# Block-sorted attention and a StarReLU feed-forward on one core: query transposes ahead of the spread product, all spread products together, scores directly behind the first value tile

## The chip, the cores and the metric

The kernel runs on one core of one Trainium2 chip. The metric is the device time of one execution in microseconds (us). The core has five engines with queues of their own: TensorE (PE, with its weight loads as PEld), VectorE (DVE), ScalarE (ACT), GpSimd (POOL) and SyncE (SP); DMA transfers are issued here from the queues of GpSimd and SyncE.

## The reference

Queries, keys and values have 4 batches, 8 heads, 768 positions and 64 elements per head. The positions form 8 blocks of 96. A small matrix `sort_net` (8 x 8 for each batch and head) is balanced by five rounds of exponentials and of divisions by row and column sums, and then mixes the blocks of keys and values. Attention runs inside each block, and its output goes through a feed-forward layer of 512 to 2048 to 512 with a squared ReLU.

```python
for _ in range(5):
    P = P - np.max(P, axis=-1, keepdims=True)
    P = np.exp(P)
    P = P / (np.sum(P, axis=-1, keepdims=True) + 1e-09)
    P = P / (np.sum(P, axis=-2, keepdims=True) + 1e-09)
k_sorted = np.einsum('bhij,bhjcd->bhicd', P, k_b).reshape(B, H, S, D)
v_sorted = np.einsum('bhij,bhjcd->bhicd', P, v_b).reshape(B, H, S, D)
...
scores = scale * np.matmul(q_b, k_sb.transpose(0, 1, 2, 4, 3))
scores = scores - np.max(scores, axis=-1, keepdims=True)
attn = np.exp(scores)
attn = attn / (np.sum(attn, axis=-1, keepdims=True) + 1e-09)
attn_out = np.matmul(attn, v_sb)
...
x = np.ascontiguousarray(attn_out.transpose(0, 2, 1, 3)).reshape(B * S, H * D)
h = x @ w_in
r = np.maximum(h, 0.0)
g = s * (r * r) + b
out = (g @ w_out).astype(np.float32)
```

## The kernel before

The order of instructions on every engine is written out by hand: each engine works through its instructions in the order in which the code issues them, and waits only for data and for free buffers. Every tile of the on-chip accumulator memory (PSUM) comes from one of two rings: `psa` with three tiles of two halves ("banks") of 512 f32 columns, and `psb` with two tiles of one bank. A tile of a ring is written again when all readers of its former use are done.

The work falls into a front, in which batch 0 is sorted and its first half (four of the eight blocks) is attended, and a long part in which the feed-forward of one half runs on TensorE while the attention of the next halves is laid into slots between its matmuls (`ffn1`, `ffn2` and their dictionaries of slots). The front, in the order of the code:

- **Loads.** SyncE issues `sort_net` and the values of batch 0 (`v0f`, four pieces). GpSimd issues the first half of the queries of batch 0 (`load_qh(0, 0)`, L104, 384 KB), the keys of batch 0 in three pieces (L93), builds `ident` and `emat`, and then issues the input weights `wi` (L140) with the second half of the queries in four pieces between them. GpSimd's later issues wait for earlier transfers to land.
- **Warm-up.** `warm(n, w, m)` (L127) is `n` matmuls of zeros with `w` columns and `m` output rows. There are 16 of 256 columns, 108 of 96 columns and 6 of 512.
- **Balancing** (L235 to L252). The five rounds run on VectorE with the exponentials on ScalarE; between them ScalarE also rearranges the values (`permute`, L194). The result is `sn`, one row for each batch and head.
- **Spread product** (L257). One f32 matmul for each batch brings the rows of `sn` to the partitions of that batch; each shows as two passes in the trace. `spread_first` does batch 0 into a tile of `psb`. `build_pd` (L271 to L286, VectorE) makes the mixing matrix `pd` from it.
- **Query transposes** (`q_banks`, L206). 48 transposes on TensorE (L216) into two tiles `tqb` of `psb`, and two evictions (one on VectorE, one on ScalarE) to `qt`.
- **Keys.** `k_piece` twice (L292, tiles `tp`) and `k_banks` (L318, tiles `tkb`), each with the mixing matrix, evicted to `ks` by VectorE and ScalarE in turn (`evac`, L202 and L204).
- **Values and scores.** `v_piece` (L328, tiles `tv`) sorts a quarter of the values and is evicted to `vs`. Behind the first comes `spread_all`: the spread products of all four batches (eight passes) into the last 128 columns of both banks of a `psa` tile `sc1`, and a copy by ScalarE to `later` (L269), from which `build_pd` of batches 1 to 3 reads. Then come `s_banks` and `s_piece`, the scores of head pairs 0 and 1 (L398, L380) with their exponentials on ScalarE (L403, L384); the scores of pair 1 go to the same tile `sc1`. Three more `v_piece` follow; the evictions of the third and fourth are cut into two halves.
- **Product with the values** (`p_piece`, L408). It takes `fill` matmuls of zeros with 240 columns (L416), eight matmuls (L422, tile `pv`), and on VectorE a reciprocal (L427) and a multiplication (L428) to `x`. `t_piece` (L433, transposes at L439) turns `x` to `xt`, with evictions on ScalarE, and `part` (L464) begins the feed-forward (L468 fills, L473 `hps`).

The second half of the queries of batch 0 is transposed in the first slot of `ffn1(0)`.

Of the kernel before, what the change touches and what calls it, by code (L numbers as in the profile page):

```python
# [9 lines left out]
FP = mybir.dt.float32  # L10
# [12 lines left out]
def kernel(  # L23
# [12 lines left out]
    nc = tc.nc  # L36

    B, H, S, D = q.shape
    NB = sort_net.shape[-1]
# [7 lines left out]
    TG = HB * BLK  # L47
# [32 lines left out]
    for c in range(0, C2, CV):  # L80
        nc.sync.dma_start(out=v0f[:, c:c + CV, :].rearrange("p c d -> p (c d)"),
                          in_=raw[2][0][:, c * D:(c + CV) * D])
# [44 lines left out]
    def warm(n, w=512, m=128):  # L127
        z = psb.tile([128, 512], FP, tag="b", name="z")
        for _ in range(n):
            nc.tensor.matmul(out=z[0:m, 0:w], lhsT=zeros[:, 0:m], rhs=zeros[:, 0:w],  # L130
                             start=True, stop=True)
# [68 lines left out]
    def evac(eng, out, in_):  # L200
        if eng == "A":
            nc.scalar.copy(out=out, in_=in_)  # L202
        else:
            nc.vector.tensor_copy(out=out, in_=in_)  # L204

    def q_banks(b, half, engs):  # L206
        if b not in QT:
            QT[b] = trp.tile([128, 2, NHP, CQ, 64], BF, tag="qt", name="qt")
        pr = slice(half * 64, (half + 1) * 64)
        for u in range(2):  # L210
            tr = psb.tile([128, 1024], BF, tag="b", name="tqb")
            for a in range(2 * u, 2 * u + 2):
                for c in range(CQ):
                    for e in range(2):
                        o = (a % 2 * CQ + c) * 64
                        nc.tensor.transpose(out=tr[e * 64:(e + 1) * 64, o:o + 64],  # L216
                                            in_=QH[b][pr, 2 * a + e, c, :],
                                            identity=ident[pr, pr])
            evac(engs[u], QT[b][:, half, 2 * u:2 * u + 2].rearrange("p a c t -> p (a c t)"),
                 tr[:, 0:2 * TG])  # L220

    idle = [
        lambda: nc.vector.tensor_reduce(
# [6 lines left out]
    nc.vector.tensor_tensor(out=sn, in0=sn, in1=rstat.broadcast_to([BH, NB, NB]),  # L230
                            op=ALU.subtract)
    warm(16, 256)
    warm(108, 96, 64)
    warm(6)
    for it in range(5):  # L235
        nc.scalar.activation(out=sn, in_=sn, func=AF.Exp)
        for c in {1: (0,), 3: (1,), 4: (2, 3)}.get(it, ()):
# [13 lines left out]
        nc.vector.tensor_tensor(out=sn, in0=sn, in1=spread(rrec, [[0, NB], list(rrec.ap[1])]),  # L251
                                op=ALU.mult)  # L252
    PD = {}
    later = const.tile([128, 2, B // 2, NB * NB], FP)

    def spread_rows(b, o):
        nc.tensor.matmul(out=o, lhsT=emat[:, b, :], rhs=sn.rearrange("p i j -> p (i j)"),  # L257
                         start=True, stop=True)

    def spread_first():  # L260
        pe = psb.tile([128, 512], FP, tag="b", name="pe")
        spread_rows(0, pe[:, 0:NB * NB])
        return pe[:, 0:NB * NB]

    def spread_all(ps):
        for b in range(B):
            o = TG + b // 2 * NB * NB
            spread_rows(b, ps[:, b % 2, o:o + NB * NB])
        nc.scalar.copy(out=later.rearrange("p u w n -> p u (w n)"), in_=ps[:, :, TG:512])  # L269

    def build_pd(b, rows):  # L271
        tmp = rtp.tile([128, NB, NB], FP, tag="tmp", name="tmp")
        nc.vector.tensor_tensor(out=tmp, in0=rows.rearrange("p (i j) -> p i j", j=NB),
                                in1=spread(jsel, [[0, NB], list(jsel.ap[1])]), op=ALU.mult)
        pt = rtp.tile([128, NB], FP, tag="pt", name="pt")
        nc.vector.tensor_reduce(out=pt, in_=tmp, axis=AX.X, op=ALU.add)
        cs = rtp.tile([128, 1], FP, tag="cs", name="cs")
        nc.vector.tensor_reduce(out=cs, in_=pt, axis=AX.X, op=ALU.add)
        rc = rtp.tile([128, 1], FP, tag="rc", name="rc")
        nc.vector.reciprocal(out=rc, in_=cs)  # L280
        pd = const.tile([128, 2, 2, NG], BF, name=f"pd{b}")
        nc.vector.scalar_tensor_tensor(
            out=pd.rearrange("p e z (a i) -> p (e z a) i", i=NB),
            in0=spread(bm, [list(bm.ap[1]), [0, NB]]), scalar=rc,
            in1=spread(pt, [[0, 4 * NHP], list(pt.ap[1])]), op0=ALU.mult, op1=ALU.mult)
        PD[b] = pd  # L286
# [79 lines left out]
    def s_piece(b, half, hp, sc=None):  # L366
        g0 = hp * NB + half * HB
        if sc is None:
            sc = psa.tile([128, 2, 512], FP, tag="a", name="sc")
        byp = len(QT[b].shape) == 5  # L370
        for n in range(HB):
            for e in range(2):
                pr = slice(e * 64, (e + 1) * 64)
                if byp:
                    o = sc[:, e, 0:TG].rearrange("p (c t) -> p c t", c=CQ)[:, :, 16 * n:16 * n + 16]
                    r = QT[b][pr, half, hp, :, 16 * n:16 * n + 16]
                else:
                    o = sc[:, e, n * BLK:(n + 1) * BLK]
                    r = QT[b][pr, half * HB + n, hp, :]
                nc.tensor.matmul(out=o, lhsT=KS[b % 2][pr, g0 + n].rearrange("p z c -> p (z c)"),  # L380
                                 rhs=r, start=True, stop=True)
        at = atp.tile([KR, 2, TG], BF, tag="at", name="at")
        if byp:
            nc.scalar.activation(out=at.rearrange("p e (t c) -> p e t c", c=CQ),  # L384
                                 in_=sc[0:KR, :, 0:TG].rearrange("p e (c t) -> p e t c", c=CQ),
                                 func=AF.Exp, scale=scale)
        else:
            nc.scalar.activation(out=at, in_=sc[0:KR, :, 0:TG], func=AF.Exp, scale=scale)  # L388
        AT[b, half, hp] = at

    def s_banks(b, half, hp):
        g0 = hp * NB + half * HB
        at = atp.tile([KR, 2, TG], BF, tag="at", name="at")
        sc = [psb.tile([128, TG], FP, tag="b", name="scb") for _ in range(2)]
        for n in range(HB):
            for e in range(2):
                pr = slice(e * 64, (e + 1) * 64)
                nc.tensor.matmul(  # L398
                    out=sc[e].rearrange("p (c t) -> p c t", c=CQ)[:, :, 16 * n:16 * n + 16],
                    lhsT=KS[b % 2][pr, g0 + n].rearrange("p z c -> p (z c)"),  # L400
                    rhs=QT[b][pr, half, hp, :, 16 * n:16 * n + 16], start=True, stop=True)
        for e in range(2):
            nc.scalar.activation(out=at[:, e].rearrange("p (t c) -> p t c", c=CQ),  # L403
                                 in_=sc[e][0:KR].rearrange("p (c t) -> p t c", c=CQ),
                                 func=AF.Exp, scale=scale)
        AT[b, half, hp] = at

    def p_piece(b, half, hp, fill=0):  # L408
        g0 = hp * NB + half * HB
        atf = AT.pop((b, half, hp)).rearrange("p e t -> p (e t)")  # L410
        if hp == 0:
            X[b, half] = xp.tile([BLK, HB, d_model], BF, tag="x", name="x")
        x = X[b, half]
        pv = psa.tile([128, 2, 512], FP, tag="a", name="pv")
        for i in range(fill):
            nc.tensor.matmul(out=pv[:, i % 2, 272:512], lhsT=zeros[:, 0:128], rhs=zeros[:, 0:240],  # L416
                             start=True, stop=True)
        for e in range(2):
            for n in range(HB):
                c0 = (e * HB + n) * BLK  # L420
                m = 128 if c0 + 128 <= 2 * TG else BLK
                nc.tensor.matmul(out=pv[0:m, e, n * VW:(n + 1) * VW],  # L422
                                 lhsT=atf[:, c0:c0 + m], rhs=VS[b % 2][:, e * NG + g0 + n, :],
                                 start=True, stop=True)
        pvv = pv[0:BLK, :, 0:HB * VW].rearrange("p e (n w) -> p e n w", w=VW)
        rec = rtp.tile([BLK, 2, HB], FP, tag="rec", name="rec")
        nc.vector.reciprocal(out=rec, in_=pvv[:, :, :, D])  # L427
        nc.vector.tensor_tensor(  # L428
            out=x[:, :, hp * 128:(hp + 1) * 128].rearrange("p n (e d) -> p e n d", e=2),
            in0=pvv[:, :, :, 0:D],  # L430
            in1=rec.unsqueeze(3).broadcast_to([BLK, 2, HB, D]), op=ALU.mult)
# [93 lines left out]
        nc.sync.dma_start(out=out[r0:r0 + 128, ns], in_=ot[:, ns])  # L525


    build_pd(0, spread_first())
    q_banks(0, 0, "DA")
    k_piece(0, 0, "D")  # L530
    k_piece(0, CK, "A")
    k_banks(0, 2 * CK, "DA")
    v_piece(0, 0, "D")
    sc1 = psa.tile([128, 2, 512], FP, tag="a", name="sc")
    spread_all(sc1)
    s_banks(0, 0, 0)
    s_piece(0, 0, 1, sc1)
    v_piece(0, CK, "D")
    v2 = v_piece(0, 2 * CK, "D", 1)
    v3 = v_piece(0, 3 * CK, "A", 1)  # L540
    v2("D")
    s_banks(0, 0, 2)
    p_piece(0, 0, 0, 3)
    v3("A")
    p_piece(0, 0, 1, 2)
    s_banks(0, 0, 3)
# [48 lines left out]
    def VRW(b, u): return lambda: v_rows(b, u)  # L595
    def VB(b): return lambda: v_back(b)
    def TD(b, h): return lambda: t_dma(b, h)
    def PDB(b): return lambda: build_pd(b, later[:, b % 2, b // 2, :])
    def QD(b): return lambda: q_dma(b)
    def LV(b): return lambda: load("v", b, 6, QT[b - 1][:, NB - 1, 0, 0:1])  # L600

# [83 lines left out]
```

## Time and profile before

| What | us |
|---|---|
| Median of three runs | 222.98 (222.55 to 224.73) |
| Profiled execution | 222.54 |
| Its span, first to last instruction | 220.4 |
| TensorE busy, share of the span | 213.6 (97%) |
| VectorE busy | 126.0 (57%) |
| ScalarE busy | 109.4 (50%) |
| GpSimd busy | 70.8 (32%) |
| Spread product of batch 0 (L257), start | 11.23 |
| First scores (L398), start | 16.52 |
| First product with values (L422), start | 20.03 |
| First `hps` matmul (L473), start | 23.13 |

The time of the execution holds some 2 us outside the span. Starts are counted from the start of the span. A busy TensorE is not TensorE at its peak, since matmuls overlap one another and a single one shows about 0.2 us from entry to end, while the next may enter 0.016 us behind it. The idle time of an engine costs something only where the chain of work that ends last runs through it.

### The profile page before, as it was taken

Reading aid. Unit: us, or ns where it says so; the run is one execution under the profiler, and the core shown is the slowest. Engines: PE = TensorE matmul, PEld = TensorE weight load, DVE = VectorE, ACT = ScalarE, POOL = GpSimd, SP = SyncE. Lnnn points to the kernel's source line nnn. Section 1 sums busy time; section 2 is a strip of 40 time slices with the busy share of each in tenths; the row PEclk is TensorE's granted clock in tenths of the full one; section 3 lists DMA queues with packets and bytes.
Section 4 is the critical chain, followed back from the end, with each engine's and each line's share of the span. In section 5 each row is a group of like instructions: output and inputs, shape, how many; then the busy total and the mean of one; then the engine's idle time right before and its main releaser. Section 6 shows DMA issues by size and latency. Waiting matters only on the chain.

```text
span 220.4 us, 5172 instructions
## 1 busy us (share of the span) xinstructions
PE 213.6 (97%) x2156; PEld 128.8 (58%) x2175; DVE 126.0 (57%) x257; ACT 109.4 (50%) x149; POOL 70.8 (32%) x127
## 2 busy tenths in 40 slices
PE   7989999999999999999999999999999999999994
PEld 5877766555465555666446555665446566654454
DVE  6777457567875768547636677547417744441222
ACT  4677687658635445664622535665424356550000
POOL 7659781689832004920050008800000000000000
PEclk9999999999999999999999999999999999999999
DMA  6999999999979662999979846999911940001212
GB/s 154 284 164 125 120 170 204 204 172 134 128 215 181 49 187 41 178 208 121 141 204 175 107 135 88 208 179 102 215 72 48 123 119 3 0 0 48 93 53 95
DMA packets 67255, 28.92 MB, mean 131 GB/s; under 512 B 51872, under 2 KB 63264, under 8 KB 67232
## 3 DMA queue, kind: packets, MB, share of 16 engines
q0 software_dynamic: 31168, 12.85, 49.5%
q1 hardware_dynamic: 36064, 15.74, 35.6%
q8 instruction: 17, 0.28, 0.6%
q14 instruction: 6, 0.05, 0.1%
HBM read 28.85 MB, written 7.86 MB: 167 GB/s over the span
## 4 chain that ended last, share of the span: by engine, by line
PE 90%; DMA 5%; DVE 1%; issue 1%; POOL 1%; ACT 0%; POOLq 0%
PE hps L473 38%; PE ops L497 36%; DMA rawk<-in_k_dram 5%; PE pv L422 4%; PE sc L380 3%; PE tpp L302 2%; PE ops L514 2%; PE tv L328 2%; PE tvr L347 1%; DVE vs L204 1%; PE tr L439 1%; PE scb L398 1%; POOL rawk L93 0%; PE sc L257 0%; PE pv L416 0%
## 5 line engine op out<-in xcount | busy, mean ns | idle before, releaser
L473 PE MATMUL hps<-xt,wi 128*128 128x384 bf16 x512 | 87.9, 326 | 0.0
L497 PE MATMUL ops<-wo,gt 128*128 128x512 bf16 x350 | 82.4, 379 | 1.4 <-issue 0.6
L485 ACT ACTIVATE rt<-hps 128x768 bf16<-128x768 f32 x64 | 51.8, 811 | 39.5 <-PE hps L473 38.3
L473 PEld LDWEIGHTS <-wi 128*128 128x128 bf16 x512 | 49.0, 98 | 32.6 <-issue 0.4
L486 DVE TENSOR_TENSOR gt<-rt 128x768 bf16<-128x768 bf16 x64 | 36.0, 565 | 41.2 <-ACT rt L485 41.0
L497 PEld LDWEIGHTS <-gt 128*128 128x128 bf16 x368 | 34.1, 98 | 37.4
L522 DVE SCALAR_TENSOR_TENSOR ot<-ops,s_bc,bias 128x512 f32<-128x512 f32 (+2 forms) x27 | 18.6, 691 | 34.7 <-PE ops L497 31.6
L388 ACT ACTIVATE at<-sc 112x768 bf16<-112x768 f32 x24 | 18.1, 808 | 30.1 <-PE sc L380 30.1
L428 DVE TENSOR_TENSOR x<-pv,rec 96x512 bf16<-96x512 f32 x32 | 22.0, 686 | 1.1
L115 POOL DMA_DIRECT2D qtok<-in_q_dram x24 | 18.6, 808 | 0.7 <-issue 0.7
L422 PEld LDWEIGHTS <-at 112*128 112x128 bf16 (+1 forms) x256 | 12.9, 101 | 6.7 <-ACT at L388 1.0
L202 ACT CAST ks<-tpp 64x512 bf16<-64x512 f32 x18 | 13.2, 731 | 4.7 <-DVE ks L204 4.1
L140 POOL DMA_DIRECT2D wi<-in_moe_w_in_dram x24 | 12.8, 558 | 5.5 <-DMA rawk<-in_k_dram 3.2
L422 PE MATMUL pv<-vs,at 112*128 112x66 bf16 (+1 forms) x256 | 13.9, 195 | 0.1
L204 DVE CAST ks<-tpp 64x512 bf16<-64x512 f32 x18 | 13.1, 729 | 0.9 <-ACT ks L202 0.5
L93 POOL DMA_DIRECT2D rawk<-in_k_dram x21 | 11.2, 550 | 2.7 <-issue 1.9
L93 POOL DMA_DIRECT2D rawv<-in_v_dram x18 | 9.7, 558 | 6.0 <-DMA wo<-in_moe_w_out_dram 4.6
L130 PE MATMUL z<-zeros 128*64 128x96 bf16 (+2 forms) x129 | 9.8, 241 | 1.3 <-DVE zeros L118 1.2
L90 POOL COPY rawk<-xt 128x1 bf16<-128x1 bf16 x2 | 0.4, 190 | 32.8 <-DMA xt<-x 32.8
L427 DVE RECIPROCAL rec<-pv 96x8 f32<-96x8 f32 x32 | 6.4, 200 | 6.4 <-PE pv L422 6.4
L130 PEld LDWEIGHTS <-zeros 128*64 128x64 bf16 (+1 forms) x130 | 7.5, 115 | 3.0 <-DVE zeros L118 1.2
L349 DVE CAST rawv<-tvr 128x512 bf16<-128x512 f32 x12 | 8.2, 683 | 0.0
(93 smaller groups left out, 137.9 us busy)
## 6 DMA issues: line engine op xcount, KB each, us to landing
out_dram<-ot SPq DMA_DIRECT2D x22, 256.0 KB, 2.6
rawv<-in_v_dram POOLq DMA_DIRECT2D x18, 128.0 KB, 5.3
rawk<-in_k_dram POOLq DMA_DIRECT2D x18, 128.0 KB, 4.1
qtok<-in_q_dram POOLq DMA_DIRECT2D x24, 96.0 KB, 6.5
wo<-in_moe_w_out_dram POOLq DMA_DIRECT2D x4, 512.0 KB, 10.8
v0f<-in_v_dram SPq DMA_DIRECT2D x4, 384.0 KB, 5.9
vd<-rawv SPq DMA_DIRECT2D x4, 384.0 KB, 6.4
vs<-vd SPq DMA_DIRECT2D x8, 192.0 KB, 8.1
```

The costliest lines, as they stand in the source:

```text
L93: nc.gpsimd.dma_start(out=ti[:, c:c + n, :].rearrange("p c d -> p (c d)"), in_=raw["qkv".index(t)][b][:, c * D:(c + n) * D])
L115: nc.gpsimd.dma_start(out=QTOK[b][:, n], in_=qv[:, n])
L130: nc.tensor.matmul(out=z[0:m, 0:w], lhsT=zeros[:, 0:m], rhs=zeros[:, 0:w], start=True, stop=True)
L204: nc.vector.tensor_copy(out=out, in_=in_)
L388: nc.scalar.activation(out=at, in_=sc[0:KR, :, 0:TG], func=AF.Exp, scale=scale)
L422: nc.tensor.matmul(out=pv[0:m, e, n * VW:(n + 1) * VW], lhsT=atf[:, c0:c0 + m], rhs=VS[b % 2][:, e * NG + g0 + n, :], start=True, stop=True)
L428: nc.vector.tensor_tensor(out=x[:, :, hp * 128:(hp + 1) * 128].rearrange("p n (e d) -> p e n d", e=2), in0=pvv[:, :, :, 0:D], in1=rec.unsq ...
L473: nc.tensor.matmul(out=H1[t, i][:, f, 0:TG], lhsT=wi[:, hp, fc:fc + 128], rhs=XT[t][:, :, hp, :], start=(hp == 0), stop=(hp == NHP - 1))
L485: nc.scalar.activation(out=rt, in_=h, func=AF.Relu)
L486: nc.vector.tensor_tensor(out=gt[:, 2 * i:2 * i + 2, :], in0=rt, in1=rt, op=ALU.mult)
L497: nc.tensor.matmul(out=ops, lhsT=gt[:, f, m * 128:(m + 1) * 128], rhs=wo[:, f, :], start=(f == 0), stop=(f == NF - 1))
L522: nc.vector.scalar_tensor_tensor(out=ot[:, ns], in0=ops, scalar=s_bc, in1=BIAS[0][:, ns], op0=ALU.mult, op1=ALU.add)
```

## The change

`q_banks` can now return its two evictions as a list of moves instead of issuing them. The 48 query transposes of the first half are issued before the balancing loop, behind a warm-up of 16 matmuls of 256 columns and 21 of 512; behind the transposes stand 16 matmuls of zeros with 128 columns into the second bank of a new `psa` tile `pe`. `spread_first` is gone: `spread_all` brings batch 0 to the first bank of `pe` and batches 1 to 3 to the second, directly one after the other, ahead of `build_pd(0)`. The query evictions follow `build_pd(0)`, as before, and ScalarE's copy to `later` follows them, with three batches instead of four. The scores of head pairs 0 and 1 come directly behind the first `v_piece`, the second in a `psa` tile of their own. The scores of pair 2 move behind the first `p_piece`, which loses its three fills.

```diff
-    def q_banks(b, half, engs):
+    def q_banks(b, half, engs, moves=None):
...
-            evac(engs[u], QT[b][:, half, 2 * u:2 * u + 2].rearrange("p a c t -> p (a c t)"),
-                 tr[:, 0:2 * TG])
+            o = QT[b][:, half, 2 * u:2 * u + 2].rearrange("p a c t -> p (a c t)")
+            if moves is None:
+                evac(engs[u], o, tr[:, 0:2 * TG])
+            else:
+                moves.append(lambda eng=engs[u], o=o, i=tr[:, 0:2 * TG]: evac(eng, o, i))
...
     warm(16, 256)
-    warm(108, 96, 64)
-    warm(6)
+    warm(21)
+    q_moves = []
+    q_banks(0, 0, "DA", q_moves)
+    pe = psa.tile([128, 2, 512], FP, tag="a", name="pe")
+    for _ in range(16):
+        nc.tensor.matmul(out=pe[:, 1, 0:128], lhsT=zeros[:, 0:128], rhs=zeros[:, 0:128],
+                         start=True, stop=True)
     for it in range(5):
...
-    later = const.tile([128, 2, B // 2, NB * NB], FP)
+    later = const.tile([128, B - 1, NB * NB], FP)
...
-    def spread_first():
-        pe = psb.tile([128, 512], FP, tag="b", name="pe")
-        spread_rows(0, pe[:, 0:NB * NB])
-        return pe[:, 0:NB * NB]
-
-    def spread_all(ps):
+    def spread_all():
         for b in range(B):
-            o = TG + b // 2 * NB * NB
-            spread_rows(b, ps[:, b % 2, o:o + NB * NB])
-        nc.scalar.copy(out=later.rearrange("p u w n -> p u (w n)"), in_=ps[:, :, TG:512])
+            o = max(b - 1, 0) * NB * NB
+            spread_rows(b, pe[:, int(b > 0), o:o + NB * NB])
...
-    build_pd(0, spread_first())
-    q_banks(0, 0, "DA")
+    spread_all()
+    build_pd(0, pe[:, 0, 0:NB * NB])
+    for mv in q_moves:
+        mv()
+    nc.scalar.copy(out=later.rearrange("p b n -> p (b n)"), in_=pe[:, 1, 0:(B - 1) * NB * NB])
     k_piece(0, 0, "D")
     k_piece(0, CK, "A")
     k_banks(0, 2 * CK, "DA")
     v_piece(0, 0, "D")
-    sc1 = psa.tile([128, 2, 512], FP, tag="a", name="sc")
-    spread_all(sc1)
     s_banks(0, 0, 0)
-    s_piece(0, 0, 1, sc1)
+    s_piece(0, 0, 1)
     v_piece(0, CK, "D")
     v2 = v_piece(0, 2 * CK, "D", 1)
     v3 = v_piece(0, 3 * CK, "A", 1)
     v2("D")
+    p_piece(0, 0, 0)
     s_banks(0, 0, 2)
-    p_piece(0, 0, 0, 3)
     v3("A")
     p_piece(0, 0, 1, 2)
     s_banks(0, 0, 3)
...
-    def PDB(b): return lambda: build_pd(b, later[:, b % 2, b // 2, :])
+    def PDB(b): return lambda: build_pd(b, later[:, b - 1, :])
```

## The prediction

> **What bounds the kernel now.** I read the page first: the share of each engine, then the chain that ended last.
>
> ```profile
> PE 213.6 (97%) x2156; PEld 128.8 (58%) x2175; DVE 126.0 (57%) x257; ACT 109.4 (50%) x149; POOL 70.8 (32%) x127
> ...
> PE 90%; DMA 5%; DVE 1%; issue 1%; POOL 1%; ACT 0%; POOLq 0%
> ```
>
> TensorE is busy for 97% of the 220.4 us span and carries 90% of the chain; 5% of the chain (11.1 us) is the wait for the last third of the first keys, all before 14.4 us. The waits of TensorE add up to 1.2 us for the zeros at the start, 0.6 us of issue, and four stalls of 0.2 to 0.5 us, none of those four after 17.1 us. So the change, which touches only the first 22 us, is worth what it moves the point at which the dense matmuls follow one another without a gap, and nothing more. I therefore went through the timeline of the front engine by engine.
>
> ```profile
> 11.23 0.40 PE L257 MATMUL pe<-sn,emat 32*128 32x64 f32 x2 [0.22 <-DVE sn L243]
> 11.57 0.95 PE L216 MATMUL tqb<-ident,qh 64*64 64x64 bf16 x48
> 12.98 1.20 PE L292 MATMUL tp<-pd,rawk 128*64 128x64 bf16 x64 [0.47 <-DVE pd L282]
> 14.36 0.69 PE L318 MATMUL tkb<-pd,rawk 128*64 128x64 bf16 x32 [0.17 <-DMA rawk<-in_k_dram]
> ...
> 15.49 1.10 PE L257 MATMUL sc<-sn,emat 32*128 32x64 f32 x8
> 16.52 0.34 PE L398 MATMUL scb<-qt,ks 64*128 64x96 bf16 x8
> 17.05 0.35 PE L380 MATMUL sc<-qt,ks 64*128 64x96 bf16 x8 [0.18 <-ACT later L269]
> 17.32 1.89 PE L328 MATMUL tv<-pd,vp 128*64 128x64 bf16 x96
> 19.15 0.34 PE L398 MATMUL scb<-qt,ks 64*128 64x96 bf16 x8
> 19.43 0.48 PE L416 MATMUL pv<-zeros 128*128 128x240 bf16 x3
> 20.03 0.43 PE L422 MATMUL pv<-vs,at 112*128 112x66 bf16 x8
> ```
>
> Columns: start, duration, engine and line, output<-inputs, shapes, count, and in brackets the idle time before and what ended it. See that the transposes (11.57) end before VectorE has built pd (TensorE waits 0.47 us for it), that tkb waits for a DMA (it landed at 14.31 by its semaphore), and that the second spread product holds TensorE for 1.10 us while the keys are already sorted. The other engines in the same stretch:
>
> ```profile
> 15.13 0.59 ACT L202 CAST ks<-tkb 128x512 bf16<-128x512 f32 x1
> 16.62 0.37 ACT L269 COPY later<-sc 128x256 f32<-128x256 f32 x1 [0.90 <-PE sc L257]
> ...
> 19.25 0.59 ACT L202 CAST vs<-tv 112x512 bf16<-112x512 f32 x1 [0.78 <-PE tv L328]
> 19.74 0.88 ACT L403 ACTIVATE at<-scb 112x384 bf16<-112x384 f32 x2
> 20.49 0.60 ACT L202 CAST vs<-tv 112x512 bf16<-112x512 f32 x1
> ```
>
> ```profile
> 18.06 2.42 DVE L204 CAST vs<-tv 112x1024 bf16<-112x1024 f32 x3 [1.24 <-PE tv L328]
> 20.49 0.20 DVE L427 RECIPROCAL rec<-pv 96x8 f32<-96x8 f32 x1
> ```
>
> ScalarE waits for the later rows and again for the last value tile; VectorE waits 1.24 us for the second value tile and then sets the start of the softmax division at 20.49. The queue of GpSimd shows when the queries arrive:
>
> ```profile
> 9.77 0.54 POOL L140 DMA_DIRECT2D wi<-in_moe_w_in_dram  x1 [1.09 <-DMA qh<-in_q_dram]
> ...
> 26.70 0.54 POOL L140 DMA_DIRECT2D wi<-in_moe_w_in_dram  x1 [1.15 <-DMA qh<-in_q_dram]
> ```
>
> The first query half was issued at 1.28 and took 8.2 us, so it lands at 9.48. The last quarter of the second half lands at 26.42 by its semaphore, and TensorE's transposes of those heads start at about 26.61.
>
> **Step 1, warm-up and transposes ahead of the spread product.** Removed: 108 narrow and 6 wide zero matmuls, which run from 4.73 to 10.85. Added: 21 of 512 columns; at the 0.216 us spacing of the six they end at 9.40 (the first 0.3 us still at half rate). Then TensorE must wait for the queries, a new wait: 9.48 + 0.05 (the gap from landing to matmul seen at tkb) = 9.53. The 48 transposes issue in 0.76 and hand over in another 0.1 (second half of the queries: 26.03 to 26.78, next matmul 26.905): 10.40. The 16 zero matmuls of 128 columns at 0.057 (the same fill in front of hps) take 0.91: 11.31. The spread product so starts at about 11.33 instead of 11.23: **+0.10 us**, because the balanced values are ready at 11.09 and now something stands in front. Behind that wait are the spread product and, through pd, everything; before, the same transposes were hidden under the 1.3 us in which VectorE builds pd, so moving them wins nothing by itself.
>
> **Step 2, all spread products at once.** Eight passes (four f32 products of two), 0.11 us apart, end at about 12.45, inside the time in which VectorE builds pd (now to 13.03). The first product and the other three lie in different halves of the tile. If VectorE waits for its own half only, pd is +0.10; if for the tile, it waits six more passes, 6 x 0.11 = 0.67. The trace shows a wait between disjoint columns of the same halves (L380 starts at 17.05, right after the copy of L269 ended at 17.00) and none that tells of different halves. I take the half, since the nearest row, L380, tells of a wait inside the same halves only. The Trainium skill, PSUM — Partial Sum Buffer, section on bank collisions, says that two engines must be kept apart by bank and not by address; the row of L380 agrees, and by that rule the other bank costs nothing here. The copy of the later rows (at most 0.37) follows ScalarE's query copy and fills the 0.31 us that it idled before the key tile: at most +0.1, hidden behind the next step. Moving on: tp 13.08 to 14.10; tkb starts at 14.36 as before, since the DMA decides. VectorE's and ScalarE's key evictions are +0.10, so the last key tile is ready at 15.82 instead of 15.72.
>
> **Step 3, scores directly behind the first value tile.** Gone from the path: 1.10 of passes and the 0.18 wait. The scores start at 15.87 (was 16.52), the second pair at 16.06 (was 17.05), the second value tile at 16.35 (was 17.32): **-0.97 there.** From there the gain shrinks. The third value tile must wait for the eviction of the first (VectorE, 15.70 + 1.23 = 16.93), the fourth for the exponentials of the second pair (ScalarE: 16.25 + 0.87 + 0.82, overlapping by 0.1 each, = 17.84), so it starts at 17.89 (was 18.53): -0.64. Its first half is evicted from 18.62 to 19.21 (was 19.85). VectorE's three evictions run from 17.09 to 19.51 (was 20.48).
>
> **Step 4, the third pair of scores behind the first product with the values.** The three fills (0.48) go, under the wait for ScalarE. The first pv starts at 19.37 (0.16 after the eviction, as now; was 20.03), the scores follow at 19.63, their exponentials at 20.01 to 20.88 (19.74 to 20.62 before: now later, since ScalarE idles from 19.21). Behind them on ScalarE stands the second half of the last value eviction: 20.78 to 21.38 (was 20.49 to 21.09). Its tile must be free before the third pv can begin, so that pv's fill starts at 21.43 where it now starts at 21.39. **The 0.66 of the first pv is gone by the third.** What remains is the fourth pair of scores, at 21.07 minus 0.14 (was 21.12); its exponential ends at 21.80 instead of 21.99, and that is what the first transpose of x waits for: 21.87 instead of 22.04, **-0.17**. The following steps keep this, as their waits are on work that moves with it (x by VectorE is 0.06 to 0.1 earlier and needed 0.6 later).
>
> **Step 5, the way to the end.** At 26.03 the second half's transposes would start 0.16 earlier, and heads 6 and 7 at 26.45; the landing at 26.42 lets them start at 26.47. It caps any gain at about 0.15, whatever the front wins, because those DMAs are issued by GpSimd in a chain of landings that this change doesn't touch. Behind it TensorE has no wait for data to the end. Sum: **-0.15 us**; with both ends of the open prices (tile wait +0.55 at the third pv by the same steps; the cap not there, if the DMAs come earlier: -0.2; the full -0.97 kept: -1.0) it is -1.0 to +0.6. The profiled execution took 222.54 in all, its span 220.4; it would be 222.4. The median of the three runs shown lies 0.44 above the profiled one, so 222.98 - 0.15 gives **222.8**. What a measurement of this kernel can tell is about 1%, 2.2 us.
>
> **Rivals.**
> *The queries are late (slower).* Place: TensorE's queue before the spread product. The transposes now stand in front, and 1.85 us (9.48 to 11.33) pass from landing to spread product. From a landing of 9.4 on, each us of delay is a us on pd, of which tkb's wait for its own DMA absorbs 0.26. At 10.4 pd is 1.0 later and the third pv about 0.75: 223.7. For: the transfer took 8.2 us where the quarters of the other half took 3.4 to 5.3, in DMA slices that are full. Against: it is the first on its queue, and a landing this late would also show in the keys.
> *VectorE waits for all eight passes.* tmp starts at 12.45 instead of 11.67, the third pv's fill at about 22.0: +0.55, 223.5. For: the wait of L380. Against: that is one within the same halves.
> *The whole gain arrives.* ScalarE takes the exponentials without its idle time and the last query quarter lands earlier: -1.0, 222.0. For: VectorE is 0.97 earlier. Against: the order on ScalarE, and 26.42.
> *The clock falls.* TensorE now idles from about 18.6 to 19.4, and around 21.3, where fills were. The clock record of the trace grants full speed from 5.0 us on; the first 16 zero matmuls of 256 columns took 0.213 each, half the rate of the later ones (240 columns in 0.10). If the half rate came back over two stretches as long as the one from 1.2 to 5.0, with the dense hps (0.16 each) at 0.33, it would cost up to 3 us: 225.6. For: removed fills. Against: 0.5 us of idle before pd now leaves the clock alone. The Trainium skill, TensorE: Matmul & The Clock Gate, section on the clock gate, puts the window at about 3.4 us; the trace's release at 5.0 us, 3.8 after the first matmul, agrees, and by that rule a gap under 1 us does nothing, though its section on a second failure mode tells of oscillation from small gaps.
>
> **How the numbers follow.** Forecast 0.64 (-0.5 to +0.3), whole gain 0.10, late queries 0.11, tile wait 0.08, clock 0.04, other 0.03. Only the clock passes 1% by its working; the three runs shown differ by 1% among themselves, so a little is left on both sides: faster 0.04, same 0.88, slower 0.08. Range 221.7 (the whole gain, and 0.3 of spread) to 224.1 (the late queries, and 0.4).
>
> **What would show it.** Right: transposes at about 9.5, spread at 11.3, tkb still at 14.36 behind the DMA, scores at 15.9, second value tile at 16.4, third pv's fill at about 21.4 behind ScalarE, first transpose of x at 21.9, heads 6 and 7 behind the landing. Wrong: tmp after 12.3, a spread product after 11.6, a granted clock below 1 after 5 us, or the second half's transposes more than 0.4 away from 25.9.

## The result and the profile after

The changed kernel takes 225.32 us in the median of 15 runs (224.02 to 227.87), where the kernel before took 222.78 (222.47 to 224.73) beside it. The ratio is 1.0101, with a 95% interval of 1.0085 to 1.0118, from the runs that a passing slow phase of the chip did not lengthen. The prediction was 222.8 with a range of 221.7 to 224.1, and a small gain. The change costs about 1%, and the time lies outside the range.

The profiled execution took 224.74 us, its span is 222.6 where it was 220.4. The page, in its parts 1, 2 and 4:

```profile
PE 213.7 (96%) x2075; PEld 127.4 (57%) x2093; DVE 126.7 (57%) x257; ACT 109.3 (49%) x149; POOL 71.2 (32%) x127
...
PEclk9988999999999999999999999999999999999999
...
PE 90%; DMA 5%; ACT 1%; DVE 1%; issue 1%; SPq 1%
```

TensorE is busy for as long as before, with 81 matmuls fewer, and its clock was lowered once in the first tenth of the span. All of the loss is in the front: the first `hps` matmul starts at 25.29 (23.13 before, +2.16), the first `ops` matmul of the long part at 52.28 (50.12, +2.16), and the span is 2.2 longer. TensorE in the front, from the timeline of the changed kernel:

```profile
11.35 1.10 PE L265 MATMUL pe<-sn,emat 32*128 32x64 f32 x8
13.80 1.20 PE L294 MATMUL tp<-pd,rawk 128*64 128x64 bf16 x64 [1.35 <-DVE pd L284]
15.22 0.99 PE L320 MATMUL tkb<-pd,rawk 128*64 128x64 bf16 x32 [0.21 <-ACT qt L202]
15.97 0.67 PE L330 MATMUL tv<-pd,vp 128*64 128x64 bf16 x17
17.05 0.59 PE L330 MATMUL tv<-pd,vp 128*64 128x64 bf16 x15 [0.41 <-issue]
17.57 0.50 PE L400 MATMUL scb<-qt,ks 64*128 64x96 bf16 x8
...
18.32 2.10 PE L330 MATMUL tv<-pd,vp 128*64 128x64 bf16 x96
21.66 0.43 PE L424 MATMUL pv<-vs,at 112*128 112x66 bf16 x8 [1.24 <-DVE vs L204]
22.02 0.34 PE L400 MATMUL scb<-qt,ks 64*128 64x96 bf16 x8
...
23.80 0.43 PE L424 MATMUL pv<-vs,at 112*128 112x66 bf16 x8
24.20 0.33 PE L441 MATMUL tr<-ident,x 96*128 96x96 bf16 x4
```

Four things are to be seen. The mixing matrix comes late, and with it the first key matmul (13.80, was 12.98). TensorE stops in the middle of a value tile, after 17 of 32 matmuls, for 0.41 us, and the view names no releaser for it ("issue"). The key tile takes 0.99 where it took 0.69, so the clock is low there. The first pv comes 1.63 later than before; VectorE is named as its releaser, but the eviction that it needs ended at 21.05, and the first weight load of pv started at 21.17: the last half microsecond, up to 21.66, is a stop between that load and its matmul, again with nothing to wait for. (Another part of the evictions ended at 21.65, but pv does not need it: in the kernel before, pv started at 20.03 and that part ended at 20.48.)

VectorE's first step of the mixing matrix stands at 12.49, and the windows of the front show the clock (columns: window, length, busy time of PE, PEld, DVE, ACT and POOL with counts, granted clock, DMA share, GB/s):

```profile
12.49 0.22 DVE L275 TENSOR_TENSOR tmp<-pe,jsel 128x64 f32<-128x64 f32 x1 [1.36 <-PE pe L265]
```

```profile
12.00:15.30 3.30, 1.74 (x74) 1.59 (x74) 2.35 (x7) 2.56 (x5) 2.11 (x5) 1.00 1.33 192
15.30:18.80 3.50, 3.09 (x99) 2.80 (x99) 2.27 (x3) 2.23 (x5) 3.29 (x8) 0.51 1.04 123
```

The clock record of the trace has the half rate from 15.36 to 18.77, right behind a stretch in which TensorE was busy for 1.74 of 3.30 us.

### The profile page after: what moved, and what is told of

It is laid out like the page before. It is cut to its first block, busy times and chain, and to the rows that moved or that the text cites. A ratio compares the mean times of both kernels' runs of the same rounds, so it can differ in the third digit from the quotient of the medians.

```text
span 222.6 us, 5010 instructions
## 1 busy us (share of the span) xinstructions
PE 213.7 (96%) x2075; PEld 127.4 (57%) x2093; DVE 126.7 (57%) x257; ACT 109.3 (49%) x149; POOL 71.2 (32%) x127
## 4 chain that ended last, share of the span: by engine, by line
PE 90%; DMA 5%; ACT 1%; DVE 1%; issue 1%; SPq 1%
PE hps L475 38%; PE ops L499 36%; DMA v0f<-in_v_dram 5%; PE pv L424 4%; PE sc L382 3%; PE tv L330 2%; PE tpp L304 2%; PE ops L516 2%; PE tvr L349 1%; DVE vs L204 1%; PE scb L400 1%; PE tr L441 1%; ACT vp L194 1%; SPq L81 1%; PE tkb L320 0%
## 5 line engine op out<-in xcount | busy, mean ns | idle before, releaser
L130 PE MATMUL z<-zeros 128*128 128x512 bf16 (+1 forms) x37 | 8.3, 405 | 1.2 <-DVE zeros L118 1.2
L405 ACT ACTIVATE at<-scb 112x384 bf16<-112x384 f32 x14 | 6.1, 487 | 2.6 <-PE scb L400 2.6
```

## The experiments

All times are against runs of the kernel before on the same chip; ratios have their 95% interval.

**A tile of its own for the product of batch 0.**

```diff
+    pe0 = psa.tile([128, 2, 512], FP, tag="a", name="pe0")
...
-            spread_rows(b, pe[:, int(b > 0), o:o + NB * NB])
+            spread_rows(b, (pe if b else pe0)[:, int(b > 0), o:o + NB * NB])
...
-    build_pd(0, pe[:, 0, 0:NB * NB])
+    build_pd(0, pe0[:, 0, 0:NB * NB])
```

> The changed kernel, but the spread product of batch 0 has a PSUM tile of its own. Theory A (VectorE's first step of the mixing matrix waits for all eight passes, because they share a tile, and this stall also lets the clock fall): tmp starts at about 11.75 instead of 12.49, pd comes 0.7 earlier, the granted clock stays at full between 5 and 25 us, and the time falls by 0.7 to 1.5 us against the changed kernel (to 223.5 to 224.5). Rival (the loss is in the order behind the values and in stalls of TensorE's instruction issue): tmp moves, the time by less than 0.4.

Measured: 223.9, ratio 1.0060 (1.0023 to 1.0097).

```profile
11.90 1.10 PE L266 MATMUL pe<-sn,emat 32*128 32x64 f32 x8
...
15.20 0.45 PE L331 MATMUL tv<-pd,vp 128*64 128x64 bf16 x17
16.91 0.41 PE L331 MATMUL tv<-pd,vp 128*64 128x64 bf16 x15 [1.26 <-issue]
...
22.36 0.43 PE L425 MATMUL pv<-vs,at 112*128 112x66 bf16 x8 [2.40 <-issue]
```

```profile
12.37 0.23 DVE L276 TENSOR_TENSOR tmp<-pe,jsel 128x64 f32<-128x64 f32 x1 [1.18 <-PE pe L266]
```

The step on VectorE now follows the start of the spread product by 0.47 us (11.90 to 12.37) and not by 1.14 (11.35 to 12.49): that wait was for all eight passes, and a tile of its own takes it away. In the trace of the changed kernel only the last of the eight passes signals; with two tiles the first product signals by itself. The profiled run is the longest of its ten (226.47): both stops are larger in it than in the changed kernel's profile, and behind the second the clock fell, from 23.29 to 26.70. The stops are at the same places: behind the 17th matmul of the first value tile and at the first pv. In seven of the ten runs the mean clock was 0.999 or more, so that it did not fall there (one fall of 3.41 us gives 0.992), and these took 223.38 to 224.20; the three others took 224.66 to 226.47. In the changed kernel it stayed up in two runs of 15.

**Zero matmuls while pd is built.**

```diff
-    k_piece(0, 0, "D")
+    k_piece(0, 0, "D", 6)   # six zero matmuls of 512 columns into its tile first
```

> The changed kernel, with six zero matmuls of 512 columns ahead of the first key matmuls, in the time in which TensorE waits for pd. tmp stays at about 12.5. Theory B (the clock falls because TensorE idles 1.4 us within one window of 3.4 us): granted clock at full behind 5 us, tkb at 0.7 instead of 1.0 us, time lower by about 0.5 us. Rival (the clock falls for another reason, or its price is hidden under other waits): the clock is as before or the time moves by less than 0.2.

Measured: 226.76, ratio 1.0168 (1.0123 to 1.0214). The theory failed as it was put: the clock stayed up where it had fallen but dropped later, from 23.01 to 26.42, and the kernel became slower still.

```profile
10.73 0.94 PE L216 MATMUL tqb<-ident,qh 64*64 64x64 bf16 x48 [0.77 <-DMA qh<-in_q_dram]
...
19.85 0.60 PE L334 MATMUL tv<-pd,vp 128*64 128x64 bf16 x27 [0.35 <-ACT at L390]
21.93 0.28 PE L334 MATMUL tv<-pd,vp 128*64 128x64 bf16 x5 [1.48 <-issue]
```

A stop of 1.48 us stands in another value tile. This run also shows the new wait for the queries: they landed at 10.69 here, and the spread product started at 12.60.

**The narrow warm-up in the changed kernel.**

```diff
-    warm(21)
+    warm(101, 106, 64)
```

> The changed kernel, with 101 zero matmuls of 106 columns and 64 rows instead of the 21 of 512: the same time of warm-up, and as many TensorE instructions ahead of the transposes as in the kernel before. Theory C (two stalls of 0.4 us in the changed kernel, 256 TensorE instructions apart, come from where blocks of instructions end): the stalls at 16.4 and 21.2 us go or move to other instructions, time lower by up to 0.8 us. Rival (they come from data or the clock): they stay at the same instructions and the time is the same within 0.3.

Measured: 224.38, ratio 1.0064 (1.0035 to 1.0093). By the ratios that is 0.8 us less than the changed kernel, with intervals that just overlap. There is no stop without a releaser left in the front: the first value tile runs its 32 matmuls in one piece (1.09 at the low clock), and the first pv starts at 20.79 instead of 21.66. Ahead of the first key matmul 189 TensorE matmuls now stand, as against 180 in the kernel before and 109 in the changed one. The clock fell all the same, from 15.09 to 18.51, behind the wait of 1.35 us for pd, which this run keeps.

**The old place of pair 2 in the changed kernel.**

```diff
-    p_piece(0, 0, 0)
     s_banks(0, 0, 2)
+    p_piece(0, 0, 0, 3)
```

> The changed kernel, with the scores of pair 2 ahead of the first product with the values again, and its three fills. Theory D (the order puts ScalarE's second eviction half behind exponentials that start late): the third product with the values starts 0.4 to 0.9 us earlier against the first, and the time falls by 0.4 to 0.9 us. Rival (that order costs nothing, as the prediction had it for ScalarE's chain): within 0.2 of the changed kernel.

Measured: 225.04, ratio 1.0106 (1.0039 to 1.0174). The first to the third pv take 1.36 us (22.58 to 23.94) instead of 2.14, as the theory said, and the time is the same: a stop of 1.28 us came in front of them, inside the scores of pair 2, and the queries were late (transposes at 10.76). With the same wait of 1.35 us for pd the clock did not fall in this profile: it is full from 6.91 on.

**The wide warm-up in the kernel before**, and nothing else of the change:

```diff
-    warm(108, 96, 64)
-    warm(6)
+    warm(27)
```

> The kernel before, with 27 zero matmuls of 512 columns in place of the 108 narrow and 6 wide ones: the same time of warm-up, 174 TensorE instructions fewer ahead of the spread product, and nothing else of the change. Theory C (TensorE stalls where a block of 256 instructions ends if it comes there before the next block has been fetched, and the narrow warm-up ran through the blocks early): stalls of 0.4 us or more without a releaser appear between 14 and 24 us, and the time rises by 0.7 to 2 us. Rival (the stalls belong to the new order): no such stall, time within 0.4 us of before.

Measured: 224.76, ratio 1.0080 (1.0063 to 1.0097). This one edit, in the kernel before, costs four fifths of the changed kernel's loss.

```profile
12.97 1.20 PE L291 MATMUL tp<-pd,rawk 128*64 128x64 bf16 x64 [0.47 <-DVE pd L281]
...
15.12 0.43 PE L256 MATMUL sc<-sn,emat 32*128 32x64 f32 x2
17.39 0.88 PE L256 MATMUL sc<-sn,emat 32*128 32x64 f32 x6 [1.84 <-issue]
```

All is much as before up to 15.12; then TensorE stops for 1.84 us inside a group of eight f32 passes. Behind it the clock falls (19.20 to 22.61). The loss is not the clock's alone: one of the four runs had a mean clock of 1.000, so no fall, and it took 224.23, 1.4 above the median before.

**The same instructions in two orders.** Both kernels are the one before, with 98 zero matmuls of 16 columns and 16 of 512 in the warm-up, so that as many instructions stand ahead of the spread product as before:

```diff
-    warm(108, 96, 64)
-    warm(6)
+    warm(98, 16, 32)      # tiny_late has these two lines
+    warm(16)              # the other way round
```

> The kernel before, with 98 zero matmuls of 16 columns and 32 rows and then 16 of 512 columns in place of the 108 narrow and 6 wide ones: the same number of TensorE instructions ahead of the spread product (130 matmuls), the many small ones first. Theory C (what counts is when TensorE passes the 193rd instruction, since the block that starts at the 449th is fetched some 2 to 4 us after that and can be used 1.4 us after the fetch): the 193rd comes at about 7 us, no stall without a releaser between 13 and 22 us, time within 0.4 us of before. Rival (wide zero matmuls themselves do the harm, by the clock or by their reads): stalls or a lower clock, and 1 us or more slower.

> The same instructions as in the run with the small ones early, in the other order: the 16 of 512 columns first, then the 98 small ones. Theory C: the 193rd instruction comes at about 10 us, the fetch at 12.5 to 13.5, the 449th instruction stalls until about 15 (0.5 to 1.5 us without a releaser, among the key or value matmuls), time 0.4 to 1.5 us above before. Rival (the number of instructions or the width decides, not their time): the same as with the small ones early, within 0.3 us.

Measured: 223.07 with the small ones first, ratio 0.9998 (0.9980 to 1.0017); 227.11 with the small ones last, ratio 1.0188 (1.0170 to 1.0206). The first view is the run with the small ones first, the second the other:

```profile
14.02 1.20 PE L292 MATMUL tp<-pd,rawk 128*64 128x64 bf16 x64 [0.47 <-DVE pd L282]
15.03 0.70 PE L318 MATMUL tkb<-pd,rawk 128*64 128x64 bf16 x32
```

```profile
13.61 1.27 PE L292 MATMUL tp<-pd,rawk 128*64 128x64 bf16 x43 [0.47 <-DVE pd L282]
16.42 0.80 PE L292 MATMUL tp<-pd,rawk 128*64 128x64 bf16 x21 [1.54 <-issue]
```

Neither the number of the instructions nor their width decides, but when TensorE gets through them. The stop was placed rightly; its price was larger than expected, since the clock fell as well, from 13.74 to 23.98. That fall began 0.9 us ahead of the stop, behind the small matmuls and the wait for pd, so this pair shows what places the stop; the 4 us between the two are the stop's and the clock's together.

**What the stops have in common.** Count TensorE's rows in the trace from the first one (weight loads, matmuls and a few semaphore instructions). Where a trace has a stop in the front, it begins behind row 449, 704 or 705 (in the last run below once more, behind 960), whatever instruction stands there. The profile's DMA part has an "instruction" queue, q8, with 16 to 17 transfers of 16 KB, one for each 256 instructions of TensorE. Set beside the stops (times at which a row starts, and at which TensorE goes on):

| Kernel | row 193 at | fetch ends | row 449 | stop until | second fetch ends | stop near row 705 until |
|---|---|---|---|---|---|---|
| before | 8.18 | 11.93 | 13.65 | none | 16.02 | none (row 705 at 17.60) |
| small ones first | 6.83 | 11.20 | 14.68 | none | 16.61 | none (18.28) |
| changed | 10.87 | 15.64 | 16.40 | 17.05 | 20.26 | 21.66 |
| own tile | 11.36 | 15.31 | 15.45 | 16.91 | 20.91 | 22.36 |
| wide in before | 12.98 | 15.96 | 15.28 | 17.39 | 20.24 | none (22.04) |
| small ones last | 10.86 | 14.92 | 14.64 | 16.41 | 19.81 | none (22.16) |
| zero matmuls for pd | 12.07 | 15.23 | 16.73 | none | 20.52 | 21.93 |
| old pair 2 | 12.09 | 15.34 | 16.85 | none | 20.53 | 21.98 |

Each stop ends 1.4 to 1.6 us after a fetch has ended. The first of the two fetches starts 2.0 to 3.8 us after TensorE has reached row 193, which is 256 rows ahead of the stop. Where TensorE arrives at the end of a block before the next is there, it stops; where the fetch was early enough, nothing is seen. Four more traces (the narrow warm-up in the changed kernel, and three runs described below) reach row 705 at 1.26 to 1.9 us after its fetch has ended and have no stop there; only with the early scores do 0.19 us pass between rows 704 and 705, up to 1.33 us after the fetch.

The Trainium skill, Runtime: NRT & Kernel Launch, section on instruction fetch mechanics, says that the instructions come in blocks of 16 KiB, 256 instructions, by a DMA queue of the sequencer, and that crossing into the next block is mostly hidden. The block agrees with the traces (16 KB in q8, stops 256 rows apart); the hiding does for the blocks behind this front, where no trace shows a stop at a block's end, and not in the front, with up to 2.1 us from row 449 to the next.

**Pair 2 alone, in the kernel before.**

```diff
+    p_piece(0, 0, 0)
     s_banks(0, 0, 2)
-    p_piece(0, 0, 0, 3)
```

> The kernel before, with only the scores of pair 2 moved behind the first product with the values and its three fills gone. Theory D (that order costs): slower by 0.3 to 0.8 us, since the exponentials of pair 2 start 0.6 us later. Rival (it costs nothing): within 0.2 us of before.

Measured: 223.34, ratio 1.0014 (0.9995 to 1.0033). The first to the third pv take 2.14 (20.14 to 22.28) instead of 1.58, and the first `hps` comes 0.64 later than before. The time is 0.3 us higher by the ratio, at the low end of what was expected, and the interval does not exclude none.

**Three things put right in the changed kernel** (own tile, narrow warm-up, old place of pair 2, by the diffs above).

> The changed kernel with three things put right together: a tile of its own for the product of batch 0, the narrow warm-up with as many instructions as before, the old place of pair 2. What is left of the change is the transposes ahead of the spread product, the products of batches 1 to 3 behind the first, and the early scores. If the three explain the loss: within 0.5 us of before or faster (222.3 to 223.4). If the wait for the queries ahead of the spread product costs as well (late queries, the rival of the prediction): 0.3 to 1.0 us above before, with the spread product later than 11.3.

Measured: 222.95, ratio 1.0018 (0.9996 to 1.0039). By the ratio 0.4 us of the loss are left, and the interval does not exclude none. In its profile the queries had landed at 9.46, but the warm-up lasted until 10.6 (the clock came up at 6.95 only), the transposes started at 10.59 and the spread product at 12.46, 1.4 after its data were ready.

**Early scores alone, in the kernel before:** product of batch 0 and warm-up as they were, the other three products directly behind it in a `psa` tile, then the transposes, and the scores directly behind the first value tile.

```diff
-    build_pd(0, spread_first())
+    first = spread_first()
+    rest = spread_rest()          # batches 1 to 3, a psa tile of their own
+    build_pd(0, first)
     q_banks(0, 0, "DA")
+    nc.scalar.copy(out=later.rearrange("p b n -> p (b n)"), in_=rest[:, 1, 0:(B - 1) * NB * NB])
...
-    sc1 = psa.tile([128, 2, 512], FP, tag="a", name="sc")
-    spread_all(sc1)
     s_banks(0, 0, 0)
-    s_piece(0, 0, 1, sc1)
+    s_piece(0, 0, 1)
```

> The kernel before, with the products of batches 1 to 3 directly behind that of batch 0 in a tile of their own, the copy behind the query evictions, and the scores directly behind the first value tile; warm-up, transposes and pair 2 stay as they were. Theory (the good part of the change is the early scores, worth up to 0.97 at the second value tile): first pv 0.4 to 0.7 us earlier than 20.03, time 0.2 to 0.6 us under before. Rival (the landing of the last query quarter or ScalarE takes it back): within 0.2 us.

Measured: 222.73, ratio 0.9993 (0.9983 to 1.0003).

```profile
16.32 0.34 PE L399 MATMUL scb<-qt,ks 64*128 64x96 bf16 x8 [0.58 <-ACT ks L202]
...
16.76 1.39 PE L329 MATMUL tv<-pd,vp 128*64 128x64 bf16 x64
...
19.69 0.44 PE L423 MATMUL pv<-vs,at 112*128 112x66 bf16 x8
```

The second value tile starts 0.56 earlier than before and the first pv 0.34, although the spread product of this execution started 0.38 late. What reaches the end is 0.2 us, which the interval does not separate from nothing. Its median is the lowest here, but it is not shown to be faster than the kernel before.

**More rows in the warm-up of that kernel.**

```diff
-    warm(108, 96, 64)
+    warm(150, 64, 64)
```

> The run with the early scores, with 150 zero matmuls of 64 columns instead of 108 of 96: 84 TensorE instructions more ahead of the spread product in about the same time. If the margin of the block fetch still limits the early scores, the first pv starts 0.2 to 0.5 us before 19.69 and the time is 0.3 to 0.7 us under before. Rival (no fetch stall is left there, and the end is set by what comes later): within 0.2 us of the run with the early scores, that is 222.4 to 222.9.

Measured: 224.05, ratio 1.0050 (1.0036 to 1.0064): slower than both cases expected.

```profile
14.90 0.61 PE L329 MATMUL tv<-pd,vp 128*64 128x64 bf16 x27
17.19 0.28 PE L329 MATMUL tv<-pd,vp 128*64 128x64 bf16 x5 [1.68 <-issue]
...
21.29 0.26 PE L417 MATMUL pv<-zeros 128*128 128x240 bf16 x1 [0.60 <-issue]
```

The first stop is at row 704 and ends 1.46 us after the second fetch ended (15.73). The second is 256 rows on, behind row 960, and ends 1.44 after the third fetch (19.85). In this profile the clock is full from 5.80 on, and in five of the six runs its mean is 0.998 or more, so the loss of about 1 us needs no fall of the clock. With 84 rows more ahead, row 449 is passed without a stop at 13.14 and the dense code behind it reaches the next block at 15.32, before its fetch has ended. More instructions early are no good by themselves: the time from block to block has to fit the fetch, each time.

## Why the prediction was wrong, point by point

- **Step 1 failed.** It priced the warm-up by its columns (21 x 0.216) and the wait for the queries, +0.10 us. Both of these came true in the profile: transposes at 9.48, spread product at 11.35 (11.33 forecast). But it let the narrow matmuls go without asking what else their rows did (the program has 162 instructions fewer, all of them TensorE's, because of the warm-up). They took TensorE through its first blocks early, so that each next block was there in time. The term was missing, and the warm-up edit alone cost a ratio of 1.0080 where +0.10 us would be 1.0004. The kernel before had little to spare: it reached row 705 at 17.60, 1.58 us after the fetch had ended (16.02), where the stops end 1.4 to 1.6 after theirs.
- **Step 2 took the wrong end of its bound.** It chose the wait for a half of the tile; tmp came at 12.49, and the rival had said 12.45. The row used for the choice (a wait inside the same halves) told nothing of different halves. The reason is not a bank: one signal is given for the run of passes into a tile. The Trainium skill's page PSUM — Partial Sum Buffer, section on bank collisions, speaks of what must be kept apart, not of when the signal comes, and did not bear on it. The runs show 0.67 us for this wait, and the ratio fell from 1.0101 to 1.0060 with it gone; the two intervals overlap.
- **Step 3 was right in direction.** With nothing else changed the second value tile starts 0.56 earlier, or 0.94 counted from the spread product (5.15 us behind it against 6.09), against -0.97 forecast. In the changed kernel this gain was in the 18.32 too, under 2 us of losses.
- **Step 4 named the right place.** The first to the third pv take 2.14 instead of 1.58 with the new order, so it loses 0.56 there; the prediction had the loss at 0.66 and set it against a gain of 0.66 at the first pv. That gain never came, and so this was a net loss, though a small one (1.0014 alone).
- **Step 5, the cap by the last query quarter,** was never reached in the changed kernel: the second half's transposes started at 28.19, and the quarter landed at 25.04.
- **The rivals.** Two of them, the wait for all passes (chance 0.08) and the clock (0.04), happened in the changed kernel's profile, one behind the other; each had been priced as if it came alone. The late queries (0.11) did not happen there: they landed at 9.43. In the five other profiles with the transposes first they landed at 9.46 to 10.71 (twice over 10.4), the transposes started at 9.81 to 10.76, and the spread product at 11.69 to 12.63, up to 1.5 us after its data; in two of them it was the warm-up that lasted longer, since the clock came up later.
- **The clock.** Its falls came behind a wait for pd (changed kernel, narrow warm-up) or a stop (own tile, zero matmuls for pd, wide warm-up before), or behind the small matmuls; but gaps as long left it up in other profiles (old pair 2, more rows). The Trainium skill, TensorE: Matmul & The Clock Gate, section on the clock gate, has a window of about 3.4 us, and the low stretches agree (3.41); that the clock falls after an idle window of such a length does not, as no gap ahead of the changed kernel's fall was over 1.4. What a fall costs by itself stays open, since the filler meant to settle it moved the stops: without a fall the own-tile runs are the faster ones, while the two such runs of the changed kernel took 224.57 and 224.72, among the others (224.02 to 226.38).
- **What is shown.** That the warm-up edit costs time through the stops is shown: alone it brings the stop and 0.8%, also in a run without a fall of the clock, and the same instructions in two orders have the stop or do not have it. How the 2.5 us between the two medians divide among stops, tile wait and clock is shown only roughly, because the parts shift one another.

## What to carry to other kernels

Zero matmuls of a warm-up have two sizes: the time for which they keep an engine busy, and the number of instructions by which they move everything behind them in the instruction stream. When a filler of a dense front is exchanged, count rows of the engine in steps of 256 (here from row 193) and look when the instruction queue's transfers end. And where an engine waits for one of several results, give that result a tile of its own, since a run of matmuls into one tile may signal once, at its end.

## What the runs showed of the hardware that was not expected

- TensorE's stop at the end of an instruction block: 0.4 to 2.1 us, ending 1.4 to 1.6 us after a 16 KB fetch whose packets took 0.9 to 1.7 us beside full data queues. The view of waits calls it "issue", or puts it down to the last engine that the stopped instruction had waited for.
- The full clock came at 4.85 to 6.95 us in the profiles, and at 9.98 in the one with the small matmuls early, though all begin with the same 16 zero matmuls; until then the wide matmuls stand 0.427 apart and not 0.216. With the transposes behind a warm-up of a fixed number of matmuls, that alone moves the transposes: to 10.03 and not 9.48 with a clock up at 6.22.
- The clock fell to one half for 3.41 us behind a stretch of 3.3 us in which TensorE was busy for only half, and for 10.24 us, three times as long, in the run with the small matmuls last, though TensorE was at work for 8.74 of the 10.30 us around it. Each fall lies a whole multiple of 3.41 us behind the time at which the clock had come up (6.83, 10.24, 13.65 or 17.07 us).

```profile
13.70:24.00 10.30, 8.74 (x239) 8.14 (x239) 4.65 (x6) 3.72 (x7) 8.78 (x16) 0.50 1.04 128
```
